# A linear-attention and MLP kernel: eight places for the MLP's turned tokens in SBUF

## The chip, the cores and the metric

The kernel runs on one core of one Trainium2 chip. The metric is the device time of one execution in microseconds (us). The time before is the median of two runs, 877.35 us (877.15 to 877.54). "TensorE", "VectorE", "ScalarE", "GpSimd" and "SyncE" are the core's engines; the profile calls them PE (with PEld for the loads of weights), DVE, ACT, POOL and SP. SBUF is the memory on the core from which the engines read; it has 128 partitions, and a place in it is given in bytes within a partition. PSUM is the memory into which TensorE writes.

## The reference, cut to what matters

Two layers, each an attention block and an MLP, over 2048 tokens of 448 features:

```python
def _A_ref(x, wqkv, wo):                      # 16 heads of 28
    qkv = (x @ wqkv).reshape(B, S, 3, H, Dh).transpose(2, 0, 3, 1, 4)
    q, k, v = qkv[0], qkv[1], qkv[2]
    phi = lambda t: jnp.where(t > 0, t + 1, jnp.exp(t)) + 1e-6
    pq, pk = phi(q), phi(k)
    kv = jnp.einsum("bhsd,bhse->bhde", pk, v)
    z = jnp.einsum("bhsd->bhd", pk)
    num = jnp.einsum("bhqd,bhde->bhqe", pq, kv)
    den = jnp.einsum("bhqd,bhd->bhq", pq, z)[..., None] + 1e-6
    return (num / den).transpose(0, 2, 1, 3).reshape(B, S, D) @ wo

def _B_ref(x, w1, b1, w2, b2):                # 448 -> 1792 -> 448
    h = _gelu(jnp.einsum("bsd,df->bsf", x, w1) + b1)
    return jnp.einsum("bsf,fd->bsd", h, w2) + b2

x = A_x
x = x + _A_ref(_layernorm(x), A_wqkv, A_wo)
x = x + _B_ref(_layernorm(x), B_w1, B_b1, B_w2, B_b2)
x = x + _A_ref(_layernorm(x), A_wqkv, A_wo)
x = x + _B_ref(_layernorm(x), B_w1, B_b1, B_w2, B_b2)
```

## The kernel before

All of it is in float32, and the large products are made from a high and a low part: a number is rounded to the type float32r (hi), the rest is kept as a second float32r number (lo), and a product is the sum of hi x hi, hi x lo and lo x hi. That is why matmuls come in threes. Of the 448 features, the first 384 make three chunks of 128. The last 64 stand twice in a fourth chunk, once for the weight's hi and once for its lo, so that the fourth chunk needs two matmuls and not three. A product over 448 features thus takes 3 x 3 + 2 = 11 matmuls.

The 2048 tokens are 16 tiles of 128, and four tiles make a block. A first phase of each layer goes over the 16 tiles and computes the attention's keys and sums; a short middle part makes one matrix of all that is needed for the queries; the second phase goes over the four blocks. In a block, `mlp1` makes one slice of 128 of the 1792 hidden features for the block's 512 tokens (11 matmuls of 512 columns), ScalarE applies the gelu and rounds (`g`, `gh`), VectorE makes the low part (`gl`), and `mlp2` multiplies the slice into four accumulators (12 matmuls of 448 columns). There are 14 such steps in a block. The program issues `mlp1` of step i+1 ahead of `mlp2` of step i. Between the two, `behind` issues what the next block needs, by a plan written out by hand (PLAN_0, PLAN_1, PLAN): the queries' part of the attention, the layer norm, the turning of the tokens by way of DRAM, and their split into hi and lo (`x0` to `x3` in the plan, `m_part` and `split_t` in the code).

The order of the instructions on each engine is that of the program, as the schedule is manual; the waits are put in by the framework, from what each instruction reads and writes.

The turned tokens of a block stand in two tiles, XH and XL (class `Block`). A tile has 2048 float32r numbers in each partition: four token tiles of 512, each with four chunks of 128 tokens. `still` gives one chunk of 128 columns, which the attention loads as weights (`proj`, L318). `moving` gives the four token tiles' runs of one chunk, which `mlp1` streams: four runs of 128 columns with 512 numbers from one start to the next. Each of XH and XL has two buffers, which attention blocks (key "a") and MLP blocks (key "m") take in turn.

```python
        def moving(self, x, c):
            return x.rearrange("p (t c n) -> p t c n", t=4, c=4)[:, :, c]

        def still(self, x, t, c):
            return x[:, (t * 4 + c) * 128:(t * 4 + c + 1) * 128]
```

In the program as built, the four buffers begin at 154112, 162304, 170496 and 178688 bytes, all multiples of 512. The weights of the first product, w1h, w1l and w1x, begin at 5888, 27392 and 48896, all 256 past a multiple of 512. The second product streams w2h and w2l (from 56064 and 81152, in steps of 1792 bytes) and loads gh and gl (256 past a multiple of 512, in steps of 512).

The first eight token tiles of the first layer are turned by TensorE instead (`TURNED`, `transpose_x`, `launch_t`). For them, `stage_n` (L406) lets ScalarE write the last 64 features twice side by side into a tile `tail` of 128 numbers with two buffers. b2b (L186), which holds the MLP's second bias in all partitions, is loaded after the first phase (L1003) and read by GpSimd in `add_bias` (L818).

Of the kernel before, what the change touches and what calls it, by code (L numbers as in the profile page):

```python
# [9 lines left out]
F32 = mybir.dt.float32  # L10
F32R = mybir.dt.float32r
# [11 lines left out]
def linear_attn_mlp_kernel(  # L23
# [19 lines left out]
    NB = NT // 4  # L43
# [8 lines left out]
    work = ctx.enter_context(tc.tile_pool(name="work", bufs=2))  # L52
# [133 lines left out]
    b2b = consts.tile([128, D], F32, name="b2b")  # L186
# [36 lines left out]


    class Block:
        def __init__(self):
            self.hi = work.tile([128, 2048], F32R, name="XH", tag="XH", bufs=2)
            self.lo = work.tile([128, 2048], F32R, name="XL", tag="XL", bufs=2)

        def pieces(self, t):  # L230

# [11 lines left out]
    blocks = {}  # L243

    def block(key):
        if key not in blocks:
            blocks[key] = Block()
        return blocks[key]

    tps = {}  # L250
# [1 line left out]
    def transpose_x(xn, tail, key, j, tag="m"):  # L252

        block(key)
        tp = tps[key, j] = bank(tag, 4 if tag == "acc" else 2, "tp")
        for c in range(4):
            pe.transpose(tp[:, c * 128:(c + 1) * 128], xn[:, c * 128:(c + 1) * 128] if c < 3 else tail, ident)

    def transpose_halves(xn, tail, key, j):

        block(key)
        tps[key, j] = [bank("acc", 4, "tp") for _ in range(2)]
        for c in range(4):
            pe.transpose(tps[key, j][c // 2][:, c % 2 * 128:][:, :128], xn[:, c * 128:(c + 1) * 128] if c < 3 else tail, ident)
# [136 lines left out]
    tails = {}  # L401
# [4 lines left out]
    def stage_n(l, t):  # L406

        xs, mv, rs = sts.pop((l, t))
        dve.tensor_scalar(xs, xs, mv[:, 0:1], rs, op0=OP.subtract, op1=OP.mult)
        xns[l, t] = xs  # L410
        if t < TURNED[l]:
            d = tails[l, t] = work.tile([128, 128], F32, name="tail", tag="tail", bufs=2)
            act.copy(d.rearrange("p (u n) -> p u n", u=2), xs[:, None, TL:].to_broadcast([128, 2, 64]))

    def stage_t(l, t):
# [5 lines left out]
    def stage_sp(l, t):  # L421
        if t >= TURNED[l]:
            block(("a", l, t // 4))
            spread(("a", l, t // 4), t % 4 // 2)
# [162 lines left out]
    def launch(za):  # L587
        for tok in LAUNCH.split():
            name, (j, *c) = tok.rstrip("0123456789"), [int(i) for i in tok if i.isdigit()]
            if name in ("ka", "qa"):  # L590
                split_hi(name[0], j, st_k if name == "ka" else st_q)
            elif name in ("kb", "qb"):
                split_lo(name[0], j, st_k if name == "kb" else st_q, pool if tok in ("kb1", "kb2", "qb0", "qb2") else dve)
            elif name in ("ha", "hb", "la", "lb"):
                split_half(("a", 0, 0), j, "ab".index(name[1]), "hi" if name[0] == "h" else "lo")
            elif name == "T":
                launch_t(j)
            elif name == "K":
                stage_k(0, j, c)
            elif name == "Q":  # L600
                stage_q(0, j, c)
            elif name == "kl":
                stage_kl(0, j, za)
            else:
                {"a": stage_a, "n": stage_n, "kp": stage_kphi, "kh": stage_kh, "s": stage_s}[name](0, j)

    def phase1(l, tr):
# [6 lines left out]
        for t in range(l == 0, NT):  # L614
            norm = NORM[l][t] if t < len(NORM[l]) else ()
            for tok in STEPS.get((l, t), STEP).split():
                if tok[1:].isdigit() and tok[0] in "anv":
                    {"a": stage_a, "n": stage_n, "v": stage_t}[tok[0]](l, int(tok[1:]))
                elif tok == "q1":
                    stage_qphi(1)  # L620
# [9 lines left out]
                elif tok == "n":  # L630
                    for u in norm:
                        stage_n(l, u)
# [360 lines left out]
    for l in range(LAYERS):  # L993
# [27 lines left out]
        for tok in ORDER.split():  # L1021
            name, j = tok.rstrip("0123456789"), int("0" + tok.lstrip("abcdefghijklmnopqrstuvwxyzQTG"))
# [6 lines left out]
        for b in range(NB):  # L1029
# [6 lines left out]
            for i in range(NF):  # L1036
# [12 lines left out]
                elif l + 1 < LAYERS:  # L1049
# [4 lines left out]
                    if i in (3, 4, 6, 7, 8):  # L1054
                        t = (3, 4, 6, 7, 8).index(i)
# [36 lines left out]
```

## Time and profile before

| What | Value |
|---|---|
| Median of the runs | 877.35 us (877.15 to 877.54) |
| Profiled execution: span from the first to the last instruction | 875.2 us |
| Profiled execution: its own time | the span's 875.2 us; none beyond it was recorded |
| Median less span | 2.15 us |
| TensorE busy | 870.1 us, 99% of the span, 4182 matmul records |
| Weight loads (PEld) busy | 772.0 us, 88% |
| VectorE, ScalarE, GpSimd busy | 491.2, 344.4 and 221.1 us (56, 39 and 25%) |
| Mean granted TensorE clock | 0.999 |
| DMA | 94.76 MB, 108 GB/s over the span |

A row of a group names the line, the engine, the operation and its tiles (out <- in), the shape and the count; behind the bar stand the busy time, the mean duration of one in ns, and the idle time of the engine just before. Matmuls overlap in such rows: the duration of one holds its way through the array, and the next starts before it has ended. How fast TensorE goes is read from the starts, which the timeline gives. A row of one line or one tile gives the shortest, median and longest duration in ns, and the first and last start.

### The profile page before, as it was taken

How to read it: one execution, taken by the hardware profiler on the slowest of the kernel's cores; microseconds unless marked ns; L12 is line 12 of the kernel's file. 1: busy time of each engine (PE TensorE's matmuls, PEld its weight loads, DVE VectorE, ACT ScalarE, POOL GpSimd, SP SyncE). 2: the span in 40 equal slices, each digit the busy share in tenths (PEclk: the TensorE clock that was granted, in tenths of full speed). 3: DMA queues.
4: the chain of work that ended last, by engine and by line, in shares of the span. 5: the costliest groups of instructions: out<-in, count | busy, mean ns of one | idle time of the engine just before them, and what ended most of it. 6: DMA issues, size and time to landing. Idle time of an engine off the chain costs nothing.

```text
span 875.2 us, 11679 instructions
## 1 busy us (share of the span) xinstructions
PE 870.1 (99%) x4182; PEld 772.0 (88%) x4182; DVE 491.2 (56%) x958; ACT 344.4 (39%) x606; POOL 221.1 (25%) x250
## 2 busy tenths in 40 slices
PE   9999999999999999999999999999999999999998
PEld 8999988888888888888899998888888888888887
DVE  7878586658455443226477876864674483433112
ACT  6776635324323322333356665332233133223221
POOL 5566532235013112012222344110220140140000
PEclk9999999999999999999999999999999999999999
DMA  5474637633313402051145543352332423111001
GB/s 160 136 239 152 207 88 210 184 93 125 133 60 105 156 0 97 1 179 49 48 141 188 166 128 106 104 182 80 110 109 91 134 71 115 49 49 43 0 1 43
DMA packets 63642, 94.76 MB, mean 108 GB/s; under 512 B 8928, under 2 KB 58720, under 8 KB 63584
## 3 DMA queue, kind: packets, MB, share of 16 engines
q1 hardware_dynamic: 63408, 93.87, 33.5%
q8 instruction: 33, 0.54, 0.3%
q14 instruction: 25, 0.20, 0.1%
q10 hardware_dynamic: 176, 0.14, 0.0%
HBM read 56.17 MB, written 34.60 MB: 104 GB/s over the span
## 4 chain that ended last, share of the span: by engine, by line
PE 98%; DVE 0%; DMA 0%; POOL 0%; issue 0%; DVEq 0%; POOLq 0%
PE y L893 10%; PE y L892 10%; PE y L891 10%; PE hp L859 9%; PE hp L860 9%; PE hp L858 9%; PE hp L861 3%; PE hp L862 3%; PE psk L326 2%; PE psq L325 2%; PE psq L327 2%; PE psq L326 2%; PE psk L327 2%; PE psk L325 2%; PE G L534 2%; PE G L535 2%
## 5 line engine op out<-in xcount | busy, mean ns | idle before, releaser
L868 DVE TENSOR_TENSOR gl<-g,gh 128x512 fp32r<-128x512 f32 x112 | 82.6, 737 | 300.0 <-ACT gh L867 300.0
L864 ACT ACTIVATE g<-hp,b1s 128x512 f32<-128x512 f32 x112 | 77.1, 688 | 406.6 <-PE hp L862 401.8
L893 PE MATMUL y<-w2h,gl 128*128 128x448 f32 x447 | 163.3, 365 | 0.0
L892 PE MATMUL y<-w2l,gh 128*128 128x448 f32 x447 | 163.3, 365 | 0.0
L891 PE MATMUL y<-w2h,gh 128*128 128x448 f32 x447 | 163.3, 365 | 0.0
L859 PE MATMUL hp<-XH,w1l 128*128 128x512 f32 x336 | 131.5, 392 | 0.0
L858 PE MATMUL hp<-XH,w1h 128*128 128x512 f32 x336 | 131.2, 391 | 0.0
L860 PE MATMUL hp<-XL,w1h 128*128 128x512 f32 x336 | 131.2, 391 | 0.0
L214 POOL TENSOR_TENSOR brs<-bve,mhalf 128x1 f32<-128x1 f32 x64 | 39.4, 616 | 283.9 <-DVE bve L212 280.8
L891 PEld LDWEIGHTS y<-w2h,gh 128*128 128x128 f32 x447 | 84.0, 188 | 9.0
L892 PEld LDWEIGHTS y<-w2l,gh 128*128 128x128 f32 x447 | 84.0, 188 | 8.3
L893 PEld LDWEIGHTS y<-w2h,gl 128*128 128x128 f32 x447 | 84.0, 188 | 6.6
L860 PEld LDWEIGHTS hp<-XL,w1h 128*128 128x128 f32 x336 | 63.1, 188 | 14.1 <-issue 0.6
L859 PEld LDWEIGHTS hp<-XH,w1l 128*128 128x128 f32 x336 | 63.1, 188 | 11.3
L858 PEld LDWEIGHTS hp<-XH,w1h 128*128 128x128 f32 x336 | 63.1, 188 | 10.8
L867 ACT CAST gh<-g 128x512 fp32r<-128x512 f32 x112 | 69.7, 622 | 3.6
L751 POOL TENSOR_TENSOR pz<-pq,zb 128x448 f32<-128x448 f32 x32 | 36.6, 1147 | 82.6 <-DVE dn L757 65.9
L445 POOL TENSOR_TENSOR xnl<-x,xnh 128x384 fp32r<-128x384 f32 x32 | 35.0, 1092 | 72.6 <-ACT xnh L444 40.6
L315 DVE TENSOR_TENSOR XL<-sp,XH 128x512 fp32r<-128x512 f32 x50 | 44.4, 893 | 4.1 <-ACT XH L314 4.1
L862 PE MATMUL hp<-XL,w1x 128*128 128x512 f32 x112 | 43.6, 389 | 0.0
L861 PE MATMUL hp<-XH,w1x 128*128 128x512 f32 x112 | 43.6, 389 | 0.0
L820 POOL TENSOR_TENSOR x<-x,b2b 128x448 f32<-128x448 f32 x32 | 42.0, 1332 | 0.0
(169 smaller groups left out, 1566.8 us busy)
## 6 DMA issues: line engine op xcount, KB each, us to landing
x<-in_A_x_dram SPq DMA_DIRECT2D x32, 224.0 KB, 3.9
pq_d<-eq SPq DMA_DIRECT2D x32, 224.0 KB, 2.8
pq<-pq_d SPq DMA_DIRECT2D x32, 224.0 KB, 3.2
sq_m<-sq SPq DMA_DIRECT2D x14, 512.0 KB, 2.8
sp<-sq_m SPq DMA_DIRECT2D x56, 128.0 KB, 2.9
x<-x_d SPq DMA_DIRECT2D x32, 224.0 KB, 3.2
sq_a<-sq SPq DMA_DIRECT2D x12, 512.0 KB, 2.9
sp<-sq_a SPq DMA_DIRECT2D x48, 128.0 KB, 2.9
```

The source lines that it names most:

```text
L315: eng.tensor_tensor(lo.rearrange("p (c i n) -> p c i n", c=4, n=32), x, f(h), op=OP.subtract)
L858: pe.matmul(o, w1h[:, c, s], x.moving(x.hi, c), start=(c == 0), stop=False)
L859: pe.matmul(o, w1l[:, c, s], x.moving(x.hi, c), start=False, stop=False)
L860: pe.matmul(o, w1h[:, c, s], x.moving(x.lo, c), start=False, stop=False)
L861: pe.matmul(o, w1x[:, s], x.moving(x.hi, 3), start=False, stop=False)
L862: pe.matmul(o, w1x[:, s], x.moving(x.lo, 3), start=False, stop=True)
L864: act.activation(g, hp, AF.Gelu_apprx_tanh, bias=b1s[:, i:i + 1])
L867: act.copy(gh, g)
L868: dve.tensor_sub(gl, g, f(gh))
L891: pe.matmul(acc[j], gh[:, s], w2h[:, i], start=first, stop=False)
L892: pe.matmul(acc[j], gh[:, s], w2l[:, i], start=False, stop=False)
L893: pe.matmul(acc[j], gl[:, s], w2h[:, i], start=False, stop=stop)
```

## The change

XH and XL become 2112 numbers long instead of 2048, and a block uses 2048 of them from a place of its own. An MLP block (layer l, block b) has hi at 16 x (4 l + b) bytes and lo 128 bytes further: hi at 0, 16, ... 112 bytes, lo at 128, 144, ... 240. Attention blocks use the place 0. To make room for the 4 x 256 bytes, the two buffers of `tail` go, and the tail copies take two pieces of 128 numbers at the start of b2b.

In the program as built, the four buffers then begin at 153088, 161536, 169984 and 178432 bytes: 0 or 256 past a multiple of 512. All other tiles stay where they were.

```diff
     class Block:
-        def __init__(self):
-            self.hi = work.tile([128, 2048], F32R, name="XH", tag="XH", bufs=2)
-            self.lo = work.tile([128, 2048], F32R, name="XL", tag="XL", bufs=2)
+        def __init__(self, at):
+            self.hi = work.tile([128, 2112], F32R, name="XH", tag="XH", bufs=2)[:, at[0]:at[0] + 2048]
+            self.lo = work.tile([128, 2112], F32R, name="XL", tag="XL", bufs=2)[:, at[1]:at[1] + 2048]
...
     def block(key):
         if key not in blocks:
-            blocks[key] = Block()
+            place = (key[1] * NB + key[2]) * 4
+            blocks[key] = Block((place, place + 32) if key[0] == "m" else (0, 0))
         return blocks[key]
...
         if t < TURNED[l]:
-            d = tails[l, t] = work.tile([128, 128], F32, name="tail", tag="tail", bufs=2)
+            d = tails[l, t] = b2b[:, t % 2 * 128:][:, :128]
             act.copy(d.rearrange("p (u n) -> p u n", u=2), xs[:, None, TL:].to_broadcast([128, 2, 64]))
```

## The prediction

> **What bounds the kernel now.** I read the page's parts 1, 2 and 4 first, to see which engine sets the end.
>
> ```profile
> span 875.2 us, 11679 instructions
> PE 870.1 (99%) x4182; PEld 772.0 (88%) x4182; DVE 491.2 (56%) x958; ACT 344.4 (39%) x606; POOL 221.1 (25%) x250
> PEclk9999999999999999999999999999999999999999
> PE 98%; DVE 0%; DMA 0%; POOL 0%; issue 0%; DVEq 0%; POOLq 0%
> ```
>
> TensorE is busy for 99% of the span, 98% of the chain that ended last is its own matmuls, and the clock is full in every slice. So the time is the number of matmuls times the distance from one start to the next. Nothing but that distance, or a new wait of TensorE, can move the end. The change adds and removes no matmul, so I read next which groups read the moved tiles, XH and XL.
>
> ```profile
> L859 PE MATMUL hp<-XH,w1l 128*128 128x512 f32 x336 | 131.5, 392 | 0.0
> L858 PE MATMUL hp<-XH,w1h 128*128 128x512 f32 x336 | 131.2, 391 | 0.0
> L860 PE MATMUL hp<-XL,w1h 128*128 128x512 f32 x336 | 131.2, 391 | 0.0
> L862 PE MATMUL hp<-XL,w1x 128*128 128x512 f32 x112 | 43.6, 389 | 0.0
> L861 PE MATMUL hp<-XH,w1x 128*128 128x512 f32 x112 | 43.6, 389 | 0.0
> ```
>
> These are the first product of the MLP: 3 x 336 + 2 x 112 = 1232 matmuls, 11 in each of 112 steps (8 blocks of 14), none of which waits (the last column). The 389 to 392 ns of one are not its cost, because they overlap; the cost is read from the starts in the timeline. These are rows of one step of the first product and of the second product before it (the start is the first column):
>
> ```profile
> 402.17 0.36 PE L891 MATMUL y<-w2h,gh 128*128 128x448 f32 x1
> ...
> 404.40 0.37 PE L893 MATMUL y<-w2h,gl 128*128 128x448 f32 x1
> 404.61 0.39 PE L858 MATMUL hp<-XH,w1h 128*128 128x512 f32 x1
> ...
> 405.53 0.39 PE L859 MATMUL hp<-XH,w1l 128*128 128x512 f32 x1
> ...
> 406.89 0.39 PE L862 MATMUL hp<-XL,w1x 128*128 128x512 f32 x1
> 407.11 0.36 PE L891 MATMUL y<-w2h,gh 128*128 128x448 f32 x1
> ```
>
> From 404.61 to 407.11 one step takes 2.50 us for its 11 matmuls; 112 steps are 280 us, 32% of the span. That is the stage in which the change acts. Once settled, six distances take 406.89 - 405.53 = 1.36 us, 226.7 ns each. The matmuls of the second product, 448 columns wide, take (404.40 - 402.17)/11 = 202.7 ns. So 64 more columns cost 24.0 ns, or 0.375 ns a column. These are the prices used below.
>
> **The change part by part.** Instructions, their order on every engine and what each waits for stay as they are; I compared the two built programs row by row, and only the names of the tail copies' tiles differ. No DMA and no queue is moved. What changes is addresses.
>
> (a) XH and XL in the MLP's blocks. `moving` hands TensorE four runs of 128 columns, 512 bytes each, 2048 bytes apart. In the program before, all four buffers begin at a multiple of 512 bytes, so every run does. After, the buffers (8448 bytes each) begin at multiples of 256, and the block adds 16 x (4 layer + block) bytes to hi and 128 more to lo. All starts stay multiples of 16. Of the eight blocks, four (odd ones) start off a multiple of 32, six off a multiple of 64, seven off a multiple of 128. Is there a row for such a read? Not one: the starts met before are these.
>
> ```profile
> L698 PE MATMUL kvp<-gt,stg x64: 257/262/262, 108.2 to 541.1; 128*112 128x112 f32 x64
> L891 PE MATMUL y<-w2h,gh x447: 362/365/369, 143.1 to 870.2; 128*128 128x448 f32 x149
> L860 PE MATMUL hp<-XL,w1h x336: 389/389/467, 138.5 to 865.9; 128*128 128x512 f32 x168
> ```
>
> The columns are shortest/median/longest ns. L698 reads moving slices 448 bytes apart, so it starts at 0, 192, 128 and 64 bytes past a multiple of 256, and all 64 lie between 257 and 262. L891 reads w2h in steps of 1792 bytes, so its starts alternate between 0 and 256 past a multiple of 512, and 447 of them lie within 7 ns. Places that are multiples of 64 therefore show no price; multiples of 16 or 32 are not shown. The cost of an unaligned run is bounded below by a gain (rival 2), above by one extra piece fetched at the streaming price (rival 1). I take nothing, the value of the nearest rows, L698's and L891's, where a change of place changed nothing.
>
> The Trainium skill's page "SBUF — State Buffer", section "Door 1: The DMA port swizzle", states that SBUF has 16-byte cachelines and that each access crossing to a new line pays a penalty. A 512-byte run covers 32 such lines from any multiple of 16, so by that rule the sum is zero too, and rival 1 has no place; no run here shows the line's size.
>
> (b) The writers of the moved tiles, and the wait that starts each layer's first product.
>
> ```profile
> L314 ACT CAST XH<-sp x52: 602/617/622, 57.3 to 793.9; 128x512 fp32r<-128x512 f32 x52
> L315 DVE TENSOR_TENSOR XL<-sp,XH x50: 672/684/1643, 58.0 to 794.7; 128x512 fp32r<-128x512 f32 x50
> L270 DVE TENSOR_TENSOR XL<-tp,XH x10: 667/680/692, 18.7 to 567.5; 128x512 fp32r<-128x512 f32 x10
> 138.17 0.40 PE L859 MATMUL hp<-XH,w1l 128*128 128x512 f32 x1
> 138.46 0.47 PE L860 MATMUL hp<-XL,w1h 128*128 128x512 f32 x1
> 138.77 0.39 PE L858 MATMUL hp<-XH,w1h 128*128 128x512 f32 x1
> ```
>
> ScalarE copies hi, VectorE subtracts lo. Their time is hidden by TensorE's second product, since the tokens for block b+1 are split at steps 8 to 11 of 14 and first read after step 13. Only at the start of each layer's MLP is the cover gone: there the distances are 290 and 310 ns instead of 227, because the last lo piece has just been written by L270. If writing to a shifted place doubled those 680 ns, each of the two layers would lose 0.68 us, 1.4 us in all; if it were free of charge, nothing. Two writers with different inputs and places stand at the same 680 ns, so I take nothing.
>
> (c) The tails. The 128 x 128 tail copies of the first eight tiles go into b2b, which is idle until the bias arrives.
>
> ```profile
> L413 ACT COPY tail<-x x8: 289/298/299, 6.6 to 41.1; 128x128 f32<-128x128 f32 x8
> L257 PE MATMUL tp<-ident,tail x6: 272/272/273, 17.8 to 51.4; 128*128 128x128 f32 x6
> L1003 SPq DMA_DIRECT2D b2b<-in_B_b_dram x1: 1588/1588/1588, 112.3 to 112.3; - x1
> ```
>
> Two halves alternate, as the two buffers did, so a copy waits for the same transpose as before. The last transpose starts at 51.4 us, the bias is issued at 112.3: 61 us of cover. Cost nothing; at most the eight copies of 298 ns could double, 2.4 us, of which ScalarE's idle 61% hides all but the first two, 0.6 us.
>
> (d) XH and XL as stationary operand in the attention's blocks, where the place is zero and only the base moves to a multiple of 256.
>
> ```profile
> L327 PEld LDWEIGHTS psk<-wk,XL x96: 186/188/189, 7.8 to 527.8; 128*128 128x128 f32 x96
> L860 PEld LDWEIGHTS hp<-XL,w1h x336: 186/188/189, 138.4 to 865.7; 128*128 128x128 f32 x168
> ```
>
> XL's loads take as long as those of w1h, which already stands at 256 past a multiple of 512: nothing, with 203 - 188 = 15 ns of cover each.
>
> Sum: 0, with -29.6 to far above as bounds from (a), +1.4 from (b), +0.6 from (c). The profiled execution's span is 875.2 us, and the median of the runs shown is 877.35, so 2.15 us lie around the span; against that the sum is 875.2 + 0 + 2.15 = 877.35.
>
> **The rivals.** The deciding size first: 2%, about what a measurement of this kernel can tell from no change, is 17.5 us, or 17.5/1232 = 14.2 ns for each matmul of the first product.
>
> Rival 1, slower: an extra piece in each run. If TensorE's read of SBUF goes in pieces wider than 16 bytes, a run that starts off a piece's boundary touches one more, four more for a matmul. Price at 0.375 ns a column: pieces of 32 bytes (8 columns) 3.0 ns a run, 12.0 ns a matmul, in 4 blocks of 154 matmuls = 616: +7.4 us, 884.7. Pieces of 64 bytes: 24.0 ns in 924 matmuls: +22.2 us, 899.5. Pieces of 128: 48 ns in 1078: +51.7 us, 929.1. It crosses the 2% when the mean over the 1232 passes 14.2 ns, for six blocks off their boundary at 4.7 ns a run (12.6 columns). For it: TensorE has no idle time to hide any of it, and no row shows a start below 64 bytes. Against it: L698, which excludes an effect at 64 against 128 or 256 in its own, slower stream.
>
> Rival 2, faster: the places part two reads that collide. While a matmul streams XH, the load of the next weights runs beside it (188 of 227 ns), and before the change both begin at a multiple of 256, always. If they meet in the same part of SBUF, a shift of 16 to 240 bytes may part them. The trace bounds the gain: at best a 512-wide matmul comes down to the 448-wide one's 202.7, 24.0 ns x 1232 = 29.6 us; half of that, 12 ns, gives 14.8 us and 862.6. Against it: the 448-wide matmuls, whose two reads stand at 0 or at 256 apart, show no difference.
> The Trainium skill's page "TensorE: Matmul & The Clock Gate", section "Back-to-back issue gap", gives N/2.4 + 2.5 ns, an estimate of 215.8 ns for 512 columns. The trace has 226.7, so 10.9 ns of each matmul are not explained by that rule, and the sum by it would be at most 13.4 us less, 863.9. The page "SBUF — State Buffer", section "Who interferes with whom", speaks against any collision: it gives TensorE two independent read ports. No run here separates them.
>
> Rival 3: the change does not reach the stream, because what counts is the place within 16 bytes, or the 2048 bytes between the runs, and neither is altered. It gives the forecast's time and stands in its chance.
>
> **How the numbers follow.** No effect: 0.56, 877.35, own range 876.0 to 879.5 (877.35 + 1.4 + 0.6, and a spread of the runs below). Rival 2: 0.11, down to 862.6; the part of it beyond 2% is 0.02. Rival 1 with 32 bytes: 0.13, 884.7. With 64 bytes: 0.12, 899.5. With 128 and more: 0.08, 929 and up. Its weight is large beside the rows against it because the trace holds no read below 64 bytes. The range leaves out the last two, 0.20: 862 to 887, the upper end being 884.7 with the 2.0 of (b) and (c). Faster by over 2%: 0.02. Within 2%: 0.56 + 0.09 + 0.13 = 0.78. Slower by over 2%: 0.12 + 0.08 = 0.20.
>
> **What the profile of the changed kernel would show.** No effect: L858 to L862 keep a median of 389 ns, a step keeps 2.50 us in all eight blocks, TensorE's busy time stays at 870. Rival 1 shows by block: with 32 bytes, steps in odd blocks last 0.13 us longer and those in even ones do not; with 64 bytes, blocks 0 of both layers keep 2.50 and six others take 2.76. Rival 2 shows as steps below 2.50 us, different from block to block. (b) would show as distances over 310 ns at the first step of each layer, (c) as a wait of the bias's DMA. What would make the prediction wrong: a unit of place that no row here varies, or a stall of another engine on the shifted tiles that reaches TensorE.

## The result and the profile after

The changed kernel takes 885.87 us (median of two runs, 885.43 to 886.30), against 877.35: a ratio of 1.0093 with a 95% interval of 1.0064 to 1.0123. It is slower by about 0.9%, within the 2% bound, and inside the stated range (862 to 887). The forecast itself was no effect, and the loss is clear of the noise. So the forecast's own case did not happen.

From the page of the changed kernel (parts 1 and 4, and two groups of part 5; the code's lines are one further on):

```profile
span 883.7 us, 11679 instructions
PE 878.5 (99%) x4182; PEld 771.6 (87%) x4182; DVE 491.2 (56%) x958; ACT 344.7 (39%) x606; POOL 221.6 (25%) x250
PE 98%; DMA 0%; DVE 0%; ACT 0%; POOL 0%; issue 0%; SPq 0%; DVEq 0%; ACTq 0%
L894 PE MATMUL y<-w2h,gl 128*128 128x448 f32 x447 | 164.1, 367 | 0.0
L860 PE MATMUL hp<-XH,w1l 128*128 128x512 f32 x336 | 132.5, 394 | 0.0
```

The span has grown by 8.5 us, and TensorE's busy time by 8.4. The other engines' busy times stand where they were (VectorE 491.2 both times), and no group of the MLP's matmuls waits. So TensorE does the same matmuls at a greater distance. The row of L894 is the surprise. It is a row of the second product. None of its operands has moved, and yet its matmuls went from 365 to 367 ns and from 163.3 to 164.1 us. This is the same group before:

```profile
L893 PE MATMUL y<-w2h,gl 128*128 128x448 f32 x447 | 163.3, 365 | 0.0
```

The starts show it better. This is a step of block 2 of the first layer in the timeline of the changed kernel (start, duration):

```profile
301.19 0.36 PE L892 MATMUL y<-w2h,gh 128*128 128x448 f32 x1
...
303.46 0.37 PE L894 MATMUL y<-w2h,gl 128*128 128x448 f32 x1
303.67 0.39 PE L859 MATMUL hp<-XH,w1h 128*128 128x512 f32 x1
...
306.00 0.40 PE L863 MATMUL hp<-XL,w1x 128*128 128x512 f32 x1
306.24 0.36 PE L892 MATMUL y<-w2h,gh 128*128 128x448 f32 x1
```

The step of 11 and 12 matmuls takes 306.24 - 301.19 = 5.05 us; before, it took 4.94 (402.17 to 407.11 in the rows shown with the prediction). The eleven of the first product take 306.24 - 303.67 = 2.57 us for 2.50. The second product's distance is (303.46 - 301.19)/11 = 206.4 ns for 202.7.

The starts of all matmuls give the plain step of each block in us, that is, one without matmuls of the queries in it:

| Layer, block | hi, lo at (bytes) | step before | step after | second product after, ns a matmul |
|---|---|---|---|---|
| 0, 0 | 0, 128 | 4.94 | 5.03 | 206.2 |
| 0, 1 | 16, 144 | 4.94 | 5.01 | 206.3 |
| 0, 2 | 32, 160 | 4.94 | 5.05 | 206.5 |
| 0, 3 | 48, 176 | 4.94 | 5.01 | 206.1 |
| 1, 0 | 64, 192 | 4.94 | 4.99 | 202.5 |
| 1, 1 | 80, 208 | 4.94 | 4.97 | 202.9 |
| 1, 2 | 96, 224 | 4.94 | 5.00 | 203.2 |
| 1, 3 | 112, 240 | 4.94 | 4.98 | 206.5 |

Added up over the whole kernel from the same starts, the first product's distances went from 281.5 to 285.3 us (+3.8), and those of the second product from 271.9 to 275.0 (+3.1). The rest is in the attention's unmoved matmuls. By stage: attention of the first layer 136.8 to 136.1, its MLP 303.7 to 308.7, attention of the second layer 126.2 to 127.9, its MLP 303.6 to 306.0; the sum of the four differences is +8.5. More than half of the loss is in matmuls that the change does not touch.

### The profile page after: what moved, and what is told of

It reads as the page before. It is cut to its first block, busy times and chain, and to the rows that moved or that the text cites. A ratio compares the mean times of both kernels' runs of the same rounds, so it can differ in the third digit from the quotient of the medians.

```text
span 883.7 us, 11679 instructions
## 1 busy us (share of the span) xinstructions
PE 878.5 (99%) x4182; PEld 771.6 (87%) x4182; DVE 491.2 (56%) x958; ACT 344.7 (39%) x606; POOL 221.6 (25%) x250
## 4 chain that ended last, share of the span: by engine, by line
PE 98%; DMA 0%; DVE 0%; ACT 0%; POOL 0%; issue 0%; SPq 0%; DVEq 0%; ACTq 0%
PE y L894 10%; PE y L892 10%; PE y L893 10%; PE hp L860 9%; PE hp L861 9%; PE hp L859 9%; PE hp L863 3%; PE hp L862 3%; PE psk L327 2%; PE psq L326 2%; PE psq L328 2%; PE psq L327 2%; PE psk L328 2%; PE psk L326 2%; PE G L536 2%; PE G L537 2%
## 5 line engine op out<-in xcount | busy, mean ns | idle before, releaser
L894 PE MATMUL y<-w2h,gl 128*128 128x448 f32 x447 | 164.1, 367 | 0.0
L894 PEld LDWEIGHTS y<-w2h,gl 128*128 128x128 f32 x447 | 83.9, 188 | 7.7
```

The lines of the kernel that those rows point to most:

```text
L894: pe.matmul(acc[j], gl[:, s], w2h[:, i], start=False, stop=stop)
```

## The experiments

Each ratio is against runs of the kernel before on the same chip, whose median lay between 876.7 and 877.2 us. Distances and steps without a row beside them are worked out from the starts of the matmuls in the run's trace.

**Are the side parts to blame?** Two runs take the change apart. In the first only the tail copies move.

```diff
-            d = tails[l, t] = work.tile([128, 128], F32, name="tail", tag="tail", bufs=2)
+            work.tile([128, 128], F32, name="tail", tag="tail", bufs=2)
+            d = tails[l, t] = b2b[:, t % 2 * 128:][:, :128]
```

> Only the tail copies go into b2b; XH and XL stay as in the kernel before, at their old places. Theory A (the places of the moving runs cost time in the first product): 877.3, within 1.5 us of the kernel before, and every step of the first product as before. Rival B (a side part of the change, the tails or the moved bases, sets TensorE off differently and the rest follows): the whole +8.5 us or a good part of it, 880 to 886.

In the second all of the change is there except the places.

```diff
-            blocks[key] = Block((place, place + 32) if key[0] == "m" else (0, 0))
+            blocks[key] = Block((0, 0))
```

> All of the change but the places: tiles of 2112 numbers, bases at 0 or 256 past a multiple of 512, tails in b2b, every block at place 0. Theory A: 877.3 within 1.5 us. Rival B: 880 to 886. If the tails cost nothing (the other run) and this one is slow, it is the bases.

The first ran at 0.9999 of the kernel before (0.9990 to 1.0009), the second at 0.9998 (0.9989 to 1.0008). Tails, longer tiles and moved bases cost nothing; Rival B falls. The places alone make the 8.5 us.

**What does a place cost by itself?** A kernel of nothing but stretches of matmuls, with the place as the only thing that varies (one execution, at a granted clock of 1.000).

```diff
+    for i in range(16):                       # mvA .. mvP
+        for k in range(48):
+            pe.matmul(o, WH[:, k % 14 * 128:][:, :128], moving(XH, i * 4, k // 3 % 4), ...)
+    for i in range(16):                       # ldA .. ldP
+        for k in range(48):
+            pe.matmul(o, WH[:, i * 4 + k % 14 * 128:][:, :128], moving(XH, 0, k // 3 % 4), ...)
+    for i in range(16):                       # coA .. coP
+        for k in range(48):
+            pe.matmul(o[:, :448], WH[:, k % 4 * 128:][:, :128], YH[:, i * 4 + k % 3 * 448:][:, :448], ...)
```

> No attention and no MLP: the output is a copy of rows of the input. TensorE runs stretches of 48 matmuls with a pause between them: mvA to mvP are 512 columns in four runs, moved by 0 to 240 bytes in steps of 16, weights at 0; ldA to ldP the same with the weights moved instead; coA to coP 448 columns in one run, moved; prA to prP with every third matmul from a second tile, that one moved; shA/syA to shI/syI four steps of 11 and 12 matmuls as in the MLP, at place 0 and then at the eight blocks' places. Theory A1 (a run off a piece's boundary fetches one more piece): mv stretches at multiples of 32 or 64 bytes take 48 x 226.7 ns = 10.9 us, the others 12 ns a matmul more, 11.5; ld flat; pr like mv. Theory A2 (what counts is the place of one read against another, weights or the matmul before): mv and ld vary alike with the shift, or mv flat at 10.9 and only pr varies, by up to 5 ns a matmul, 0.25 us a stretch. Rival B: all of mv, ld, pr flat within 0.1 us, co flat at 48 x 202.7 = 9.7 us, and the steps alike for all nine places.

Groups of its page, 48 matmuls each; the number to read is the busy time behind the bar, since a stretch runs without a pause:

```profile
L73 PE MATMUL ldA<-XH,WH 128*128 128x512 f32 x48 | 11.1, 390 | 0.0
L68 PE MATMUL mvE<-XH,WH 128*128 128x512 f32 x48 | 11.2, 393 | 0.0
L73 PE MATMUL ldM<-XH,WH 128*128 128x512 f32 x48 | 11.2, 392 | 0.0
L68 PE MATMUL mvK<-XH,WH 128*128 128x512 f32 x48 | 11.5, 397 | 0.0
L73 PE MATMUL ldG<-XH,WH 128*128 128x512 f32 x48 | 11.5, 397 | 0.0
L68 PE MATMUL mvP<-XH,WH 128*128 128x512 f32 x48 | 11.6, 401 | 0.0
L78 PE MATMUL coA<-YH,WH 128*128 128x448 f32 x48 | 10.1, 369 | 0.0
L78 PE MATMUL coE<-YH,WH 128*128 128x448 f32 x48 | 9.8, 363 | 0.0
L78 PE MATMUL coK<-YH,WH 128*128 128x448 f32 x48 | 9.8, 364 | 0.0
```

ldA has both reads at 0. In mvE the streamed run stands 64 bytes further. In ldM it is the weights that stand 192 bytes further, which is the same distance seen the other way, within 256 bytes; the two rows agree. So do mvK (the stream at 160) and ldG (the weights at 96). Settled distances from the starts (the mean of the last 24 in a stretch): 226.7 ns with both at 0, 228.9 in mvE and ldM, 234.3 in mvK and ldG, 236.7 in mvP (the stream at 240). All seven pairs at multiples of 32 agree within 0.1 ns. At odd multiples of 16 the two ways differ by 0 to 3.4 ns. The 512-wide stream is never faster than with both at 0, and no place off zero is free: between 228.3 and 236.7 ns. In the pr stretches, where only every third matmul was moved, the settled distances are 226.7 ns at 0 and 228.9 to 235.5 elsewhere; 48 bytes on every third matmul (prD, 235.5) cost more than 48 bytes on all of them (mvD, 233.3), a first sign that a neighbour at another place counts too. For 448 columns it is otherwise: 206.7 ns at 0, and 200.0 at 64 and at 160, the shortest of the sixteen.

A1 falls: the stretches at multiples of 64 (mvE, mvI and mvM, 228.9, 232.1 and 233.3 ns) are no more free than those at other places, so the loss does not sort by boundaries. The first half of A2 is right in kind, larger than its 5 ns: what counts is the place of the streamed read against that of the weights loaded beside it. (All weights of a stretch stand at one place, so it does not tell a matmul's own weights from the next one's, whose load runs beside it.) A last part of the map ran four steps of 11 and 12 matmuls at the eight blocks' places. At seven of the eight its unmoved second product settled at the distance that the same block shows in the changed kernel, about 203 or about 206 ns, and its whole settled step agrees with that block's plain step within 3 ns (5.05 us at the places of block 0, 2, for instance). At the places of block 0, 0 it did not: 202.6 ns for 206.2, and 4.95 to 4.97 us for 5.03.

**Does it hold in the kernel?** All MLP blocks at one place, and then the weights moved along with them.

```diff
-            blocks[key] = Block((place, place + 32) if key[0] == "m" else (0, 0))
+            blocks[key] = Block((40, 40) if key[0] == "m" else (0, 0))
```

> The changed kernel with one place for all: every MLP block has hi and lo 160 bytes into their tiles. Theory C (what counts is the place of the streamed read against the weights loaded beside it, within 256 bytes): the map's 234.3 ns for 160 bytes against 226.7, 7.6 ns x 1232 = 9.4 us: 886; if the unmoved matmuls of the second product fall into the slower of their two rhythms (206.6 ns for 202.65), up to 6.4 us more: 886 to 893. Rival D (each block's own place off a boundary of 32 or 64 bytes): 160 is a multiple of 32 and not of 64, so 877 with pieces of 32 bytes, 906 with pieces of 64 (24 ns in all 1232).

```diff
+    pad1 = wts.tile([128, 40], F32, name="pad1")
     w1h = wts.tile([128, 3, F], F32R, name="w1h")
     w1l = wts.tile([128, 3, F], F32R, name="w1l")
     w1x = wts.tile([128, F], F32R, name="w1x")
+    pad2 = wts.tile([128, 24], F32, name="pad2")
```

> As the run with 160 bytes, and the weights of the first product (w1h, w1l, w1x) stand 160 bytes further too, so that the streamed read and the load stand again at the same place within 256 bytes. Theory C: the whole loss is gone, 876.7 within 1.5 us, and the settled distance is 226.7 ns again. Rival D: no change from the run with 160 bytes. Rival E (any change of place sets TensorE into a slower rhythm at the start): like the run with 160 bytes, or anything between.

With X alone at 160 bytes the kernel takes 883.38 us, a ratio of 1.0069 (1.0050 to 1.0088): a loss of 6.2 us, all of it in the first product (287.8 us for 281.5), and not Theory C's 9.4. Rival D with pieces of 32 bytes (877) and of 64 (906) is off by more. With the weights moved along it does not come back: 886.08, 1.0100 (1.0085 to 1.0115). Theory C, as I had put it, is refuted on the total. The timelines say where. X alone at 160:

```profile
404.61 0.36 PE L892 MATMUL y<-w2h,gh 128*128 128x448 f32 x1
...
406.84 0.36 PE L894 MATMUL y<-w2h,gl 128*128 128x448 f32 x1
407.04 0.40 PE L859 MATMUL hp<-XH,w1h 128*128 128x512 f32 x1
...
408.91 0.40 PE L861 MATMUL hp<-XL,w1h 128*128 128x512 f32 x1
```

The same step with w1 at 160 too (lines shifted by five):

```profile
402.67 0.40 PE L864 MATMUL hp<-XH,w1h 128*128 128x512 f32 x1
...
403.83 0.39 PE L866 MATMUL hp<-XL,w1h 128*128 128x512 f32 x1
...
404.96 0.39 PE L868 MATMUL hp<-XL,w1x 128*128 128x512 f32 x1
405.19 0.37 PE L897 MATMUL y<-w2h,gh 128*128 128x448 f32 x1
...
406.84 0.37 PE L899 MATMUL y<-w2h,gl 128*128 128x448 f32 x1
```

In the first, eight distances of the first product take 408.91 - 407.04 = 1.87 us, 233.8 ns each, and the second product keeps (406.84 - 404.61)/11 = 202.7. In the second, the first product is back once settled, (404.96 - 403.83)/5 = 226 ns, and 229.2 over its eleven against 228.0 before. But now the unmoved second product runs at (406.84 - 405.19)/8 = 206.3 ns. Over the kernel its distances add up to 277.0 us for 271.9. So moving the weights along does take the first product's loss away, 287.8 to 282.6 us of 281.5; the second product, whose neighbour's places now differ from its own by 160 bytes, loses as much. That a matmul's place matters to its neighbours is what I take Theory C to have left out; the run with everything moved, below, is the test. I call it Theory F from here: only places against each other count, inside one matmul and from one matmul to the next.

**The other product moved instead.** The kernel before, with w2h and w2l at 64 and at 160 bytes. Here, in the run above with w1 moved and in the next kernel, small statistics of the queries stand in the padding to make room; the diffs leave that out.

```diff
+    pad1 = wts.tile([128, 16], F32, name="pad1")     # 64 bytes; 40 for 160 bytes
     w2h = wts.tile([128, NF, D], F32R, name="w2h")
     w2l = wts.tile([128, NF, D], F32R, name="w2l")
+    pad2 = wts.tile([128, 48], F32, name="pad2")     # 24
```

> The kernel before with w2h and w2l 64 bytes further, all other tiles at places within 256 bytes as before; small statistics of the queries stand in the padding to make room. Theory C by the map's row for 448 columns moved by 64 bytes: 200.0 ns instead of 202.65 in the 1341 matmuls of the second product, 3.6 us less: 873.2 (a ratio of 0.996). Rivals D and E: 876.7 or slower.

> The same with w2h and w2l 160 bytes further. Theory C by the map's row for 448 columns moved by 160 bytes, 200.0 ns: 873.2 again, although 160 bytes is a bad place for the first product. Rival D: a run off a piece's boundary of 64 bytes, slower, 32 bytes: no change.

At 64 bytes the kernel is faster than before, 0.9979 (0.9969 to 0.9988), 2.1 us and not 3.6: the second product takes 269.1 us for 271.9, and the first product 282.9 for 281.5, as its first matmuls after the hand-over got slower. At 160 bytes it is unchanged, 1.0003 (0.9994 to 1.0013): the second product's gain (271.0) and the first product's loss (282.8) meet. The row of the map for 160 bytes did not carry over; it was measured without neighbours at another place.

**Everything moved together, and the map of steps.**

```diff
+    pad1 = wts.tile([128, 40], F32, name="pad1")
     w1h = wts.tile([128, 3, F], F32R, name="w1h")
```

> The kernel before with every tile from w1h on 160 bytes further, so that no place changes against another within 256 bytes (only ident, ones and small constants stay). Theory F (only places of reads against each other count, those of one matmul and of its neighbours): 877.0 within 1.5 us, first product 228.0 ns and second 202.7 on the mean, as before. Rival D (a run's own place off a boundary of 64 bytes costs): 905. Rival E (any place off zero sets TensorE into the slower rhythm): second product at 206.5 ns as in the run in which X and w1 alone stood 160 bytes further, 882 to 886.

With all tiles 160 bytes further the kernel takes what it took: 1.0006 (0.9997 to 1.0016), the first product at 227.9 to 228.1 ns in every block and the second at 202.6 to 202.8. In its timeline ten distances of the second product take 404.85 - 402.82 = 2.03 us and the next eleven matmuls 407.56 - 405.06 = 2.50 us, as before the change:

```profile
402.82 0.37 PE L896 MATMUL y<-w2l,gh 128*128 128x448 f32 x1
...
404.85 0.37 PE L897 MATMUL y<-w2h,gl 128*128 128x448 f32 x1
405.06 0.39 PE L862 MATMUL hp<-XH,w1h 128*128 128x512 f32 x1
...
407.56 0.36 PE L895 MATMUL y<-w2h,gh 128*128 128x448 f32 x1
```

A run's own place off a boundary of 64 bytes costs nothing, at the one shift that was run; Rivals D and E fall. Together with the run that moved X and w1 alone this is the clearest result of the study: X and w1 at 160 against w2 and gh at 0 lose 8.9 us, all of them at 160 lose nothing that can be measured.

> No attention and no MLP: the output is a copy of rows of the input. Four steps of 11 and 12 matmuls for each of 64 pairs of places: shAA/syAA to shHH/syHH, where X and w1 stand at 0, the second product's streamed weights at 0 to 224 bytes (first letter, steps of 32) and its loaded tokens at 0 to 224 bytes (second letter). Then three rounds of the attention's three elevens for 3 x 8 pairs of places (ak, ag, aq: first letter the streamed read 0, 64 or 160 bytes past the loaded one, second letter the place of the turned tokens). Theory F: the second product's distance falls into families by the difference of the two letters (200.0 for 64 or 160 bytes, 202.7 or 206.7 for none), and the same difference at another pair of places changes only the first product's first distances and the choice between two rhythms, by up to 4 ns a matmul. Theory C alone (only the pair inside one matmul): the same difference gives the same distance wherever the pair stands.

Its elevens stand at one place throughout; only the second product's two operands move (one execution, at a granted clock of 1.000). The first product's starts (L77 begins a triple, and these rows begin a step) in the stretches AA and AG:

```profile
44.69 0.39 PE L77 MATMUL shAA<-XH,WH 128*128 128x512 f32 x1
...
54.57 0.39 PE L77 MATMUL shAA<-XH,WH 128*128 128x512 f32 x1
```

```profile
170.09 0.39 PE L77 MATMUL shAG<-XH,WH 128*128 128x512 f32 x1
...
179.88 0.39 PE L77 MATMUL shAG<-XH,WH 128*128 128x512 f32 x1
```

Two steps take 9.88 us at AA, where all stand at 0 as in the kernel before, and 9.79 at AG, where the loaded tokens stand at 192, that is, the stream 64 bytes past them. Over the 64 pairs, from the starts, a step takes 4.893 us (AG) to 5.027 (CB), a spread of 2.7% from places alone; AA, with 4.940, is among the better ones. With a difference of 64 bytes the second product takes 199.8 to 201.1 ns at all eight pairs. With none it takes 201.8 to 202.7 at six pairs and 206.2 and 206.7 at two. With 160 it ranges from 200.5 to 206.3, so here my expectation of a family was wrong: 64 is sturdy, 160 is not. And the first product, whose own places never change, ranges from 226.5 to 232.7 ns with the place of its neighbour, 6 ns and not up to 4. In the attention's elevens, a stream 64 bytes past the load gives 200.0 to 200.8 ns at all eight places; no difference gives 202.6 to 206.7. Two of the 64 pairs stand at the places of the two runs that moved w2: 4.927 us at CA and 4.953 at FA, and the plain steps of those two kernels take 4.927 and 4.953 us. So the step measured as a whole did carry over, where the row for one product alone had not.

**A version that beats both.** From the maps: every 448-wide stream 64 bytes past its load, the first product's two reads at the same place.

```diff
+    pad(16)                                    # wk, wq at 64
     split_hi("k", 0, st_k)
+    pad(48)                                    # X back at 0
     stage_n(0, 0)
...
     launch_t(0)
+    pad(16)                                    # the other wk, wq at 64
...
         if (l, t) == (0, 0):
+            pad(32)                            # gh, gl, xnh, xnl at 192
         h = t512("A", 2, "xnh", F32R)
         lo = t512("B", 2, "xnl", F32R)
+            pad(32)                            # the last of wq at 64
...
+            pad(48)                            # kh, kl at 0
         kh = t512("E", 2, "kh", F32R)[:, :D]
```

> The kernel before with places chosen from the two maps; nothing else changes, instructions and order on every engine are its own (the tail copies stand in b2b, which made no difference alone). X, w1, w2 and the tiles of kh and kl stay at 0, the tiles of gh, gl, xnh and xnl stand at 192, those of wk and wq at 64. So every 448-wide matmul streams 64 bytes past the place that its neighbour's load reads. Theory F by the map's row for that pair of places: a step of 11 and 12 takes 4893.3 ns for 4940.0, 46.7 ns x 112 = 5.2 us; the attention's elevens at 200.6 for 202.7 to 203.5 ns, about 1.2 us and 1.5 us in the two layers; the queries' matmuls 264 x 2.3 = 0.6 us; sum 8.5 us, 868.4 (ratio 0.990). Theory C alone: the second product at 200.0 and the first at 228.0, 1344 x 2.7 = 3.6 us from the MLP and the rest alike, 870. Rival E (a place off zero costs): 880 or more.

It takes 871.26 us, a ratio of 0.9931 to the kernel before (0.9917 to 0.9944), and is faster than both. Its timeline, and the first steps of its first MLP:

```profile
400.24 0.36 PE L902 MATMUL y<-w2h,gh 128*128 128x448 f32 x1
...
402.43 0.36 PE L904 MATMUL y<-w2h,gl 128*128 128x448 f32 x1
402.64 0.39 PE L869 MATMUL hp<-XH,w1h 128*128 128x512 f32 x1
...
405.13 0.36 PE L902 MATMUL y<-w2h,gh 128*128 128x448 f32 x1
```

```profile
137.45 0.40 PE L870 MATMUL hp<-XH,w1l 128*128 128x512 f32 x1
138.43 0.47 PE L871 MATMUL hp<-XL,w1h 128*128 128x512 f32 x1 [0.58 <-DVE XL L275]
```

The step is 405.13 - 400.24 = 4.89 us, as the map has it, with 2.49 us for the eleven and (402.43 - 400.24)/11 = 199.1 ns between the twelve. The gain is 5.6 us and not the expected 8.5, by the stages: the two MLPs give 3.8 of 5.8, the two attentions 1.9 of 2.7. The last two rows show one place where it went: TensorE now comes to the first MLP 0.7 us earlier than VectorE's last low part, and stands from 137.45 to 138.43 for a matmul that took 0.29 us before. What else is missing was not followed up.

## Why the prediction was right or wrong

**What bounds the kernel.** Right. The time went with the distance between TensorE's starts and with nothing else, and the price of the MLP's steps could be read from them. What was wrong is the next sentence, that the stage of the 1232 matmuls is where the change acts: the second product alone lost 3.1 us, with operands that stand still.

**Part (a), nothing for the places.** This is the step that failed. I took "the value of the nearest rows, L698's and L891's, where a change of place changed nothing". In both rows the places do change, but within a matmul not against each other: L698 slices its streamed and its loaded operand by the same 448 bytes, and L891's steps of 1792 bytes differ from its loaded tokens by 0 or 256. The map's pairs at multiples of 32 bytes show a cycle of 256 bytes and that the difference counts, and the run with all tiles at 160 bytes that the place itself does not; so these rows kept the decisive quantity constant within each matmul, and in L891 at zero. They were not near at all. At odd multiples of 16 bytes the same difference cost up to 3.4 ns more or less by which of the two was moved, so there the difference is not all, and what else counts stays open. In the place of "nothing" the first product measured +3.8 us, and its neighbours +4.7.

**Rival 1** gave 884.7 with pieces of 32 bytes, close to the 885.87 measured, and that is a coincidence. It said that odd blocks lose 0.13 us a step and even ones nothing; the four even blocks lost 0.09, 0.11, 0.05 and 0.06. The run with all tiles at 160 bytes refutes pieces of 64 bytes; the map, where no multiple of 32 off zero is free, and X alone at 160 bytes (883.38 us for 877) refute those of 32 as the cause.

**What the pages gave.** The rule of the Trainium skill on 16-byte lines ("SBUF — State Buffer", section "Door 1: The DMA port swizzle") gave zero and does not cover what happens: whatever the line's size, places at multiples of 16 cost up to 10 ns a matmul. The two independent read ports that the same page gives TensorE ("Who interferes with whom") do not show in these runs either, as a stream slows by 7.6 ns when only the weights loaded beside it stand elsewhere (ldG against ldA). The estimate of 215.8 ns for 512 columns, by the formula N/2.4 + 2.5 ns that the Trainium skill's "TensorE: Matmul & The Clock Gate", section "Back-to-back issue gap", gives for the isolated gap, was not reached: no place in the map came below 226.7.

**Rival 2** had the right pair, the stream against the load beside it, and the wrong sign: places that are equal within 256 bytes are the best for the first product, not a collision to be parted. Its argument against itself (no difference at 0 or 256 apart) was right and for the same reason.

**Parts (b), (c) and (d), nothing each.** Right: the first distances of each layer's first product are 296 and 309 ns in the first layer and 310 and 302 in the second, for 291 to 307 before; the tails and the bases alone ran at 0.9999 and 0.9998.

**The range and the chances** held, by the width that the unknown price had given them: within 2% had 0.78. The case that came true, a loss of 1% spread over moved and unmoved matmuls alike, was in none of them.

## What to carry to other kernels

When TensorE is busy all the time with float32r matmuls, the place of the streamed tile against the place of the weights being loaded, within 256 bytes, is worth up to 4% of a matmul's time, and a step's neighbours count too; measure the step as a whole in a small kernel and choose tile places from that. A row only bounds an unknown effect if it varies the quantity that decides; ask of each "nearest row" what it holds constant, and here two operands sliced alike held it constant. And do not add up a change over the matmuls it touches alone: a matmul stream carries its rhythm on into the next.

## What was not expected of the hardware

In the changed kernel the unmoved matmuls of the second product ran in one of two rhythms, about 203 or about 206 ns for 448 columns, by the places of the matmuls before them; the map of steps, with more places, has values in between. The slower one lasted from the first MLP far into the next layer's attention, whose uninterrupted stretch of 452 matmuls ran at 206.7 ns for 202.7 before, at places that had not moved against each other; that stage lost 1.7 us. The run with X and w1 at 160 bytes, whose second product is slow too, shows the same stretch at 206.7 ns; the run with X alone at 160, whose second product keeps 202.7, shows it at 202.7. Why a difference of 64 bytes is good for 448 columns in one run and none for 512 in four, and what in SBUF has the cycle of 256 bytes, these runs do not say.
